# Third unit's rows loaded at the start, and quarters of the values projection between groups of transposes

## The chip, the cores and the metric

One core of a Trainium2 chip. The metric is the device time of one execution in microseconds; lower is better. PE is TensorE, DVE is VectorE, ACT is ScalarE, POOL is GpSimd, SP is SyncE, which here issues DMAs.

## The reference

Four layers on a sequence of 2048 rows of 640 numbers: attention, feed-forward, attention, feed-forward, with the same weights twice. All tensors are float32.

```python
def _A_ref(x, wqkv, wo):          # 32 heads of 20, window W = 256
    q, k, v = split heads of x @ wqkv
    scores = einsum("bhqd,bhkd->bhqk", q, k) * Dh ** -0.5
    scores = where(0 <= i - j < W, scores, -1e9)
    return merge heads of softmax(scores) @ v, then @ wo

def _B_ref(x, w1, b1, w2, b2):    # F = 1536
    r = relu(x @ w1 + b1)
    return (r * r) @ w2 + b2

x = x + _A_ref(layernorm(x)); x = x + _B_ref(layernorm(x))
x = x + _A_ref(layernorm(x)); x = x + _B_ref(layernorm(x))
```

## The kernel before

The sequence is cut into units of 256 rows (two blocks of 128), eight for each pair of layers, 16 in all, numbered u. Products are made from two float16 halves of each operand, in three matmuls (`mm3`): high by high, high by low, low by high.

For one unit the steps are these. `ln_load(u)` issues two loads of 128 rows from SP's queue and posts the layernorm's steps (statistics on DVE, the power on POOL, the scaling on DVE). `ln_t(u)` transposes the normalised rows on PE: `split_t` does one block in two groups, of three and two transposes of 128 columns, and each group is evicted by a cast on ACT (line 377) and a subtraction on DVE (line 378) into the two halves of yT. From the third unit's successors on another way is used (`ln_cross`, transposes by DMA). `stage_qk(u)` projects Q and K, evicts them on ACT and DVE (lines 507 and 510) and writes them to memory and back (lines 542 to 549), so that they come to lie by head pairs. `stage_v(u, which)` projects V in four quarters (two blocks by two halves of the columns), 15 matmuls each, and evicts each by one ACT instruction (line 580).

Attention goes in quads of four heads, eight for a unit. `max_quad` makes products and their row maxima (DVE, line 633), `max_out` transposes the maxima and sends them to rows of Q by DMA (lines 721 to 727, 689), `exp_quad` makes the products again with the maxima taken off, exponentials on ACT (line 779) and masks on POOL, and `pv_quad` multiplies by V. Maxima and exponentials use the same six PSUM banks, `bb`. `load_o(u)` fetches the result, and `stage_o` projects it (input `od`); `stage_f` is the feed-forward.

All other products share two PSUM buffers with the tag "mm" (`mm_tile`), so that a tile waits for the eviction of the tile before last.

The order on every engine is written by a planner in the kernel's own code. It keeps a clock for each engine; steps are generators that yield the time of what they put on PE, `post` and `dma` queue the work of the other engines with a cost and a priority (0 first), and `pump` puts what could start by then. A DMA is counted with its bytes over a rate (335, later 250 bytes per ns) behind all bytes counted so far. Weight loads issued by ACT (`bulk`) start when the counted backlog is under 2.2 us.

The first unit's attention is set out by `flow`: it goes through a list of maxima ("m"), rows ("r"), exponentials ("s") and products with V ("v"), and as long as the next entry isn't ready by the planner's clock, it takes a piece of the generator `rest`, which is `ahead_all()`. What `flow` has not used of `rest` is left for the second unit's part: 9 us of it by the planner's count are held back until the first `stage_o` has begun, for use between later steps.

The tiles with the tag "xt" (two buffers) hold the rows of a unit and, later, other rows. Those with the tag "x1" (two buffers) hold the input rows to which the first projection's result is added; `load_o` fills them (line 886). The second unit's yT lies in a part of the third K tile (`place`).

Of the kernel before, what the change touches and what calls it, by code (L numbers as in the profile page):

```python
# [10 lines left out]
F32 = mybir.dt.float32  # L11
# [5 lines left out]
P = 128  # L17
Q = P // 2
S = 2048
D = 640  # L20
# [25 lines left out]
def kernel(ctx: ExitStack, tc: tile.TileContext, x, wqkv, wo, w1, b1, w2, b2, out):  # L46
# [4 lines left out]
    sb = ctx.enter_context(tc.tile_pool(name="sb", bufs=1))  # L51
# [43 lines left out]
    def set_row(i, k):  # L95
        nc.vector.memset(krow[i][:, 512 * k:512 * (k + 1)], PAIR)
# [36 lines left out]
    def post(eng, cost, fn, *deps, wait=0.0, prio=1, **kw):  # L133

        j = Job(eng, cost, fn, [d for d in deps if d is not None], now[0] + wait, prio, **kw)
        k = len(pend)
        while k and pend[k - 1].prio > prio:
            k -= 1
        pend.insert(k, j)
        return j  # L140

    def bulk(fn, size, *deps, **kw):

        return post("A", 400.0, fn, *deps, prio=2, size=size, idle=True, land=WLAND, **kw)

    def dma(fn, size, *deps, n=1, cost=450.0, prio=1, **kw):

        return post("S", n * cost, fn, *deps, prio=prio, size=size, **kw)
# [18 lines left out]
    def need(*js):  # L167

        for j in js:
            while j.end is None:  # L170
                pass_time()
            now[0] = max(now[0], j.end)
# [55 lines left out]
    def mm_tile(shape, name):  # L228


        while len(banks2) > 1:
            empty = [b for b in banks2 if b and all(j.end is not None for j in b)]
            if empty:
                b = min(empty, key=lambda b: max(j.end for j in b))
                now[0] = max(now[0], max(j.end for j in b) + LAT)
                banks2.remove(b)
            else:
                pass_time()
        t = ps.tile(shape, F32, name=name, tag="mm", bufs=2)
        banks2.append([])  # L240
        return t, banks2[-1]
# [15 lines left out]
    def convert(st, hi, low, n, load, *deps, prio=2):  # L257

        a = post("A", 20 + 0.9 * n, lambda: nc.scalar.activation(hi, st, AF.Copy, scale=WS), load, *deps, prio=prio)
        return post("D", 30 + 1.04 * n, lambda: nc.vector.scalar_tensor_tensor(low, st, WS, hi, op0=ALU.mult,  # L260
                                                                               op1=ALU.subtract), a, prio=prio)
# [20 lines left out]
    def load_wo():  # L282

        v = wo.rearrange("(h c d) n -> d h c n", c=KC, d=4)
        raw = w2raw[:, (FC - KC) * D:].rearrange("p (c n) -> p c n", n=D)
        loads = []
        for d in range(4):
            loads.append(bulk(lambda d=d: nc.scalar.dma_start(raw[d * H:(d + 1) * H], v[d]), H * KC * D * 4, gate0))
        for c in range(KC):
            woj[c] = convert(raw[:, c], wo_s[:, 0, c], wo_s[:, 1, c], D, loads[-1], *loads[:-1])  # L290
        rowset[1] = [post("D", 460, lambda k=k: set_row(1, k), prio=2) for k in range(4)]
# [30 lines left out]
    def mm3(acc, lhs, rhs, nk, ns, then=None):  # L322

        k, t = 0, 0.0
        for c in range(nk):
            for a, b in ((0, 0), (0, 1), (1, 0)):
                nc.tensor.matmul(acc, lhs(a, c), rhs(b, c), start=(k == 0), stop=(k == 3 * nk - 1))  # L327
                k += 1
                t += ns
                if t >= STEP and k < 3 * nk:  # L330
                    yield t
                    t = 0.0
        if then is not None:
            then(t)
        yield t
# [31 lines left out]
                                                           op0=ALU.subtract, op1=ALU.mult), j, prio=prio)  # L367
        return j

    def split_t(y, dst, job, made, bb=None):  # L370


        yield Want(job, bank=False)
        need(job)

        def out(tr, jobs, c0, n, wait):
            j = post("A", 170 * n, lambda: nc.scalar.copy(dst[:, 0, c0:c0 + n], tr[:, :n]), wait=wait, prio=0)  # L377
            j = post("D", 170 * n, lambda: nc.vector.tensor_sub(dst[:, 1, c0:c0 + n], tr[:, :n], dst[:, 0, c0:c0 + n]), j,  # L378
                     prio=0)
            jobs.append(j)  # L380
            made.append(j)

        parts = []
        for k, (c0, n) in enumerate(((0, 3), (3, 2))):
            if bb is not None:
                tr, jobs = bb[:, k].rearrange("p (c n) -> p c n", n=P), bbjobs
            else:
                yield Want()
                tr, jobs = mm_tile([P, 4, P], "tr")
            for c in range(n):  # L390
                nc.tensor.transpose(tr[:, c, :], y[:, (c0 + c) * P:(c0 + c + 1) * P], ident)
            parts.append((tr, jobs, c0, n, 117 * n if bb is None else 117 * KC))
            if bb is None:
                out(*parts.pop())
                yield 117 * n
        if parts:
            for p in parts:
                out(*p)
            yield 117 * KC
# [3 lines left out]
    def xsrc(l, b):  # L403
        return x_rows[b * P:(b + 1) * P, :] if l == 0 else xs[b]
# [4 lines left out]

    lns = {}  # L410

    def ln_load(u, *deps, prio=2):

        l, g = divmod(u, NG)
        ys = []
        for i in range(2):
            xt = sb.tile([P, D], F32, name="xt", tag="xt", bufs=2)
            load = dma(lambda xt=xt, i=i: nc.sync.dma_start(xt, xsrc(l, 2 * g + i)), P * D * 4, *deps, prio=min(prio, 1))
            ys.append((xt, layernorm(xt, xt, load, prio=prio)))
        lns[u] = ys  # L420

    def ln_t(u, yT=None):
        ys = lns.pop(u)
        if yT is None:
            yT = sb.tile([P, 2, KC, T], F16, name="yT", tag="yT", bufs=1)
        yTs[u], pre[u] = yT, []
        bb = banks() if u == 0 else (None, None)
        for i in range(2):
            yield from split_t(ys[i][0], yT[:, :, :, i * P:(i + 1) * P], ys[i][1], pre[u], bb[i])

    def cross(ys, dst, room, prio=2):

# [34 lines left out]
    pre = {}  # L467
# [99 lines left out]
    def stage_v(u, which=range(4)):  # L567
        yT = yTs[u]
        for i in range(2):
            if u == 2:  # L570
                yield Want(sums[i], bank=False)
            vt = vts[(2 * u + i) % 6][0]
            for h in range(2):
                if 2 * i + h not in which:
                    continue
                yield Want()
                acc, jobs = mm_tile([P, 2 * T], "acc")
                need(*[wqj[c] for c in range((2 * D + h * HD) // P, (2 * D + (h + 1) * HD - 1) // P + 1)])
                def out(vt=vt, acc=acc, h=h):
                    nc.scalar.activation(vt[:, h * NP:(h + 1) * NP, 0:DH],  # L580
                                                 acc[:, :HD].rearrange("p (h d) -> p h d", d=DH),
                                                 AF.Copy, scale=1.0 / (YS * WS))

                yield from mm3(acc[:, :HD], lambda a, k: yT[:, a, k, i * P:(i + 1) * P],
                               lambda b, k: wq_s[:, b, k, 2 * D + h * HD:2 * D + (h + 1) * HD], KC, 136,
                               lambda wait: jobs.append(post("A", 320, out, wait=wait, prio=urgency["out"])))
# [11 lines left out]
    def banks():  # L598
        need(*bbjobs)
        bbjobs.clear()  # L600
        return bb6
# [251 lines left out]
    x1s, ys, y2s = {}, {}, {}  # L853
# [336 lines left out]

    spin(14)
    ln_load(0, prio=0)
    load_wq()
    run(ln_t(0))
    spin(7)
    rate[0] = 250.0
    ln_load(1)
    load_wo()
    load_w1()
    load_w2()  # L1200
# [3 lines left out]
    place = kts[2].rearrange("p a n -> p (a n)")[:, :2 * KC * T].rearrange("p (a c n) -> p a c n", a=2, n=T)  # L1204

    def ahead_all():
        yield from stage_qk(0)
        yield from stage_v(0, range(2))
        yield from ln_t(1, place)
        ln_load(2)  # L1210
        yield from stage_v(0, range(2, 4))
        yield from stage_qk(1)
        yield from ln_t(2)
        yield from stage_v(1)
        gate2.end = now[0]
        yield from stage_qk(2)
        yield from stage_v(2)

    rest = ahead_all()
    todo = [("m", n) for n in range(GQ)] + [("r", 0)] + [("m", n) for n in range(GQ, LEAD)]  # L1220
    for n in range(NQ):
# [61 lines left out]
```

## Time and profile before

| | |
|---|---|
| median of 3 runs | 1586.9 us (1585.45 to 1589.74) |
| profiled execution | 1589.08 us, span 1587.4 us |
| mean granted clock of PE | 0.997 |
| busy PE, DVE, ACT, POOL | 1556.4, 984.3, 733.9, 600.2 us |
| moved by DMA | 160.44 MB |

A line of the instructions in order of time gives the start, the time to the end of the group, engine, line, operation, output<-inputs, shape and count, and in brackets how long the engine was idle before and what ended that. In the busy time by stretch each engine's number in brackets is its count of instructions. Busy time counts instructions from start to end; a share over the whole span mixes stages that have different limits, so the stages are read one by one.

### The profile page before, as it was taken

The numbers are of one execution on the slowest core, as the hardware profiler recorded it, in microseconds if no ns is written. First come the engines' busy times: TensorE is split into PE (matmuls) and PEld (weight loads), VectorE is DVE, ScalarE is ACT, GpSimd is POOL, SyncE is SP. The second block draws the span as 40 slices with busy tenths as digits, with TensorE's granted clock in tenths as the row PEclk, the third lists the DMA queues.
The fourth block names the chain that finished last, engine by engine and source line by source line (L and its number), as shares of the span: only waits on it lengthen the run. The fifth ranks groups of instructions, "written<-read, shape, count | busy, mean of one in ns | idle before, by whom it ended". The sixth has DMA issues, their size and how long they took to land. (4 is left out here: it accounts for less than half of the span.)

```text
span 1587.4 us, 52465 instructions
## 1 busy us (share of the span) xinstructions
PE 1556.4 (98%) x21534; PEld 1167.0 (74%) x21534; DVE 984.3 (62%) x3253; ACT 733.9 (46%) x1593; POOL 600.2 (38%) x1291
## 2 busy tenths in 40 slices
PE   8989999999999999999999999999999999999999
PEld 7666767777777777778777777777777777776767
DVE  8777665656756656665566656557665666756431
ACT  4555445444453444535343453544545345454612
POOL 1234434234252433525323352442535235253612
PEclk9999999999999999999999999999999999999999
DMA  9864344362533525354352534434343353431120
GB/s 265 208 181 105 77 110 87 101 128 52 121 87 106 108 61 133 70 125 86 97 132 59 119 87 116 98 88 110 71 123 83 98 117 69 107 87 58 29 67 18
DMA packets 243209, 160.44 MB, mean 101 GB/s; under 512 B 91160, under 2 KB 226712, under 8 KB 242968
## 3 DMA queue, kind: packets, MB, share of 16 engines
q1 hardware_dynamic: 236600, 147.58, 39.3%
q10 hardware_dynamic: 6368, 9.50, 2.1%
q8 instruction: 169, 2.77, 0.8%
q14 instruction: 72, 0.59, 0.1%
HBM read 84.68 MB, written 52.95 MB: 87 GB/s over the span
## 5 line engine op out<-in xcount | busy, mean ns | idle before, releaser
L779 ACT ACTIVATE pt<-bb 128x512 f32<-128x512 f32 (+1 forms) x736 | 375.9, 601 | 226.4 <-PE bb L757 203.2
L633 DVE CUSTOM_DVE_ANT_0 bb<-bb,maskq 128x320 f32<-128x320 f32 x896 | 409.3, 523 | 89.7 <-PE bb L653 76.1
L794 POOL TENSOR_SCALAR_AFFINE_SELECT pt<-pt 128x256 f32<-128x256 f32 x448 | 188.6, 423 | 564.1 <-ACT pt L779 550.9
L327 PE MATMUL acc<-y,w_s 128*128 128x256 f16 x2880 | 330.0, 274 | 2.5 <-ACT y L377 1.4
L327 PE MATMUL acc<-w_s,hh 128*128 128x320 f16 x2304 | 326.0, 299 | 0.0
L327 PEld LDWEIGHTS <-w_s 128*128 128x128 f16 x2880 | 277.3, 98 | 55.2 <-issue 17.9
L327 PEld LDWEIGHTS <-hh 128*128 128x128 f16 x2304 | 220.6, 98 | 98.1 <-issue 11.5
L327 PEld LDWEIGHTS <-wq_s 128*128 128x128 f16 x2400 | 229.5, 98 | 46.5 <-issue 13.9
L327 PE MATMUL acc<-yT,wq_s 128*128 128x256 f16 x2250 | 258.7, 273 | 2.7 <-DVE qd L510 1.3
L798 POOL TENSOR_SCALAR_AFFINE_SELECT pt<-pt 128x256 f32<-128x256 f32 x512 | 213.6, 439 | 90.5 <-ACT pt L779 88.8
L1013 DVE TENSOR_TENSOR hh<-r,hh 128x256 f16<-128x256 f32 x192 | 95.0, 517 | 211.1 <-ACT hh L1010 204.1
L828 PE MATMUL pv<-pt,vt 128*32 128x128 f32 (+1 forms) x3840 | 190.1, 331 | 1.2 <-POOL pt L798 1.2
L1007 POOL TENSOR_TENSOR r<-r 128x256 f32<-128x256 f32 x192 | 114.3, 616 | 162.1 <-ACT r L1003 159.8
L840 ACT COPY ot<-pv 128x256 f32<-128x256 f32 x128 | 47.6, 372 | 269.3 <-PE pv L828 269.3
L327 PE MATMUL acc<-wo_s,od 128*128 128x320 f16 x960 | 140.4, 302 | 5.0 <-ACT od L911 3.0
L633 DVE DVE_READ_ACCUMULATOR2_ANT mx<- 128x1 f32 x1024 | 142.7, 139 | 0.0
L828 PEld LDWEIGHTS pv<-pt,vt 128*32 128x32 f32 x3840 | 105.2, 110 | 41.5 <-POOL pt L798 7.2
L327 PE MATMUL acc<-wq_s,yT 128*128 128x320 f16 x900 | 131.8, 299 | 1.0 <-DVE y L378 0.5
L327 PEld LDWEIGHTS <-od 128*128 128x128 f16 x960 | 91.6, 98 | 50.2 <-issue 6.4
L1003 ACT ACTIVATE r<-acc,b1s 128x256 f32<-128x256 f32 x192 | 80.5, 471 | 89.4 <-PE acc L327 88.1
L327 PEld LDWEIGHTS <-yT 128*128 128x128 f16 x900 | 85.7, 98 | 38.9 <-issue 6.3
L364 POOL TENSOR_TENSOR bmv<-bmv,neghalf 128x1 f32<-128x1 f32 x64 | 44.9, 708 | 137.4 <-DVE bmv L358 136.9
(95 smaller groups left out, 1224.4 us busy)
## 6 DMA issues: line engine op xcount, KB each, us to landing
qt<-qk SPq DMA_DIRECT2D x30, 480.0 KB
kt<-qk SPq DMA_DIRECT2D x30, 480.0 KB
qk<-qd SPq DMA_DIRECT2D x17, 640.0 KB
o<-ot SPq DMA_DIRECT2D x256, 42.0 KB
od<-o SPq DMA_DIRECT2D x14, 640.0 KB
qk<-yl SPq DMA_DIRECT2D x13, 640.0 KB
qk<-qd SPq DMA_DIRECT2D x17, 320.0 KB
xt<-in_A_x_dram SPq DMA_DIRECT2D x16, 320.0 KB
```

Source lines behind the costliest of these rows:

```text
L327: nc.tensor.matmul(acc, lhs(a, c), rhs(b, c), start=(k == 0), stop=(k == 3 * nk - 1))
L364: j = post("G", 520, lambda: nc.gpsimd.tensor_tensor(box["mv"][:, 3:4], box["mv"][:, 2:3], neghalf, op=ALU.pow), j, prio=prio)
L633: nc.vector.tensor_tensor_reduce(out=v, in0=v, in1=mask, scale=1.0, scalar=-3.0e38, op0=ALU.add, op1=ALU.max, accum_out=accum[e, w]),
L779: nc.scalar.activation(box["pt"][:, :o], bb[e][:, k, :o], AF.Exp, scale=SCALE / (QS * QS))
L794: nc.gpsimd.affine_select(out=m, in_=m, pattern=[[0, 2], [-1, P]], compare_op=ALU.is_gt, fill=0.0, base=0, channel_multiplier=1)
L798: nc.gpsimd.affine_select(out=m, in_=m, pattern=[[0, 2], [1, P]], compare_op=ALU.is_ge, fill=0.0, base=0, channel_multiplier=-1)
L828: nc.tensor.matmul(pv[32 * jj:32 * (jj + 1), q0 * P:(q0 + qn) * P], vf[:, c:c + 32], pj[:, j, :], start=(k == 0), stop=(k == len(steps) - ...
L840: nc.scalar.copy(ot[:, qd % 2], pv)
L1003: nc.scalar.activation(box["r"], acc[:, f, :], AF.Relu, bias=b1s[:, f0 + f:f0 + f + 1], scale=1.0 / (YS * WS))
L1007: nc.gpsimd.tensor_tensor(box["r"], box["r"], box["r"], op=ALU.mult)
L1013: nc.vector.tensor_sub(hh[:, 1, f, :], box["r"], hh[:, 0, f, :])
```

## The change

`split_t` gets a list of generators, `between`, and runs one behind each group of transposes. `ln_t` hands two of the list to each block. `ln_load` takes the tag of its tiles. The third unit's rows (u = 2) are loaded directly after the second's, into the tiles with the tag "x1", and their layernorm is posted there. In `ahead_all` only the first quarter of the first unit's values stands ahead of the second unit's transposes; the other three stand between these, and the four quarters of the second unit's values stand between and behind the third unit's transposes.

```diff
--- before.py
+++ after.py
@@ -367,7 +367,7 @@
                                                            op0=ALU.subtract, op1=ALU.mult), j, prio=prio)
         return j
 
-    def split_t(y, dst, job, made, bb=None):
+    def split_t(y, dst, job, made, bb=None, between=()):
 
 
         yield Want(job, bank=False)
@@ -393,6 +393,8 @@
             if bb is None:
                 out(*parts.pop())
                 yield 117 * n
+                for g in between[k:k + 1]:
+                    yield from g
         if parts:
             for p in parts:
                 out(*p)
@@ -409,24 +411,24 @@
 
     lns = {}
 
-    def ln_load(u, *deps, prio=2):
+    def ln_load(u, *deps, prio=2, tag="xt"):
 
         l, g = divmod(u, NG)
         ys = []
         for i in range(2):
-            xt = sb.tile([P, D], F32, name="xt", tag="xt", bufs=2)
+            xt = sb.tile([P, D], F32, name="xt", tag=tag, bufs=2)
             load = dma(lambda xt=xt, i=i: nc.sync.dma_start(xt, xsrc(l, 2 * g + i)), P * D * 4, *deps, prio=min(prio, 1))
             ys.append((xt, layernorm(xt, xt, load, prio=prio)))
         lns[u] = ys
 
-    def ln_t(u, yT=None):
+    def ln_t(u, yT=None, between=()):
         ys = lns.pop(u)
         if yT is None:
             yT = sb.tile([P, 2, KC, T], F16, name="yT", tag="yT", bufs=1)
         yTs[u], pre[u] = yT, []
         bb = banks() if u == 0 else (None, None)
         for i in range(2):
-            yield from split_t(ys[i][0], yT[:, :, :, i * P:(i + 1) * P], ys[i][1], pre[u], bb[i])
+            yield from split_t(ys[i][0], yT[:, :, :, i * P:(i + 1) * P], ys[i][1], pre[u], bb[i], between[2 * i:2 * i + 2])
 
     def cross(ys, dst, room, prio=2):
 
@@ -1195,6 +1197,7 @@
     spin(7)
     rate[0] = 250.0
     ln_load(1)
+    ln_load(2, tag="x1")
     load_wo()
     load_w1()
     load_w2()
@@ -1205,13 +1208,10 @@
 
     def ahead_all():
         yield from stage_qk(0)
-        yield from stage_v(0, range(2))
-        yield from ln_t(1, place)
-        ln_load(2)
-        yield from stage_v(0, range(2, 4))
+        yield from stage_v(0, range(1))
+        yield from ln_t(1, place, [stage_v(0, [k]) for k in (1, 2, 3)])
         yield from stage_qk(1)
-        yield from ln_t(2)
-        yield from stage_v(1)
+        yield from ln_t(2, None, [stage_v(1, [k]) for k in range(4)])
         gate2.end = now[0]
         yield from stage_qk(2)
         yield from stage_v(2)
```

## Prediction

> **What bounds the kernel now.** I read the page's totals first, then the busy time by stretch, and only then the instructions in order of time, where the stretches left something to find.
>
> ```profile
> span 1587.4 us, 52465 instructions
> PE 1556.4 (98%) x21534; PEld 1167.0 (74%) x21534; DVE 984.3 (62%) x3253; ACT 733.9 (46%) x1593; POOL 600.2 (38%) x1291
> ```
> ```profile
> 30.00:70.00 40.00, 35.03 (x336) 24.98 (x335) 31.67 (x130) 19.15 (x42) 7.49 (x15) 1.00 0.82 204
> 70.00:105.00 35.00, 32.09 (x418) 22.14 (x418) 24.38 (x88) 20.99 (x45) 9.26 (x20) 1.00 0.75 208
> 105.00:125.00 20.00, 14.76 (x155) 10.16 (x155) 17.86 (x52) 7.38 (x16) 4.75 (x8) 0.83 0.79 182
> ...
> 250.00:1350.00 1100.00, 1099.98 (x15642) 828.59 (x15634) 681.42 (x2271) 511.55 (x1116) 433.50 (x942) 1.00 0.42 97
> ```
>
> The columns are the stretch and its length, then the busy time of PE, PEld, DVE, ACT and POOL, the granted clock, the DMA share and GB/s. Over the 1100 us from 250 on PE is idle for 0.02 us: nothing can be won there. The change acts between 30 and 105, where PE is idle for 4.97 + 2.91 us. Behind it lies the worst stretch, 105 to 125: 5.24 us idle and a mean clock of 0.83. These three hold 13.1 us of idle time, 0.8% of the span, and that caps what an edit here can bring, apart from the clock.
>
> The instructions of PE in order of time (start, duration, idle before) show who ends the waits:
>
> ```profile
> 32.39 0.49 PE L668 MATMUL bb<-kt,qt 60*128 60x128 f16 x7 [1.32 <-DMA kt<-qk]
> ...
> 34.59 0.44 PE L391 MATMUL tr<-ident,xt 128*128 128x128 f32 x2 [0.33 <-ACT vt L580]
> 35.59 0.80 PE L391 MATMUL tr<-ident,xt 128*128 128x128 f32 x5 [0.56 <-DVE kt L378]
> ...
> 37.30 2.74 PE L327 MATMUL acc<-wq_s,yT 128*128 128x320 f16 x19 [0.47 <-DVE kt L378]
> ...
> 47.36 0.49 PE L765 MATMUL bb<-qt,kt 62*128 62x256 f16 x7 [0.75 <-DVE bmv L357]
> ...
> 61.66 0.50 PE L765 MATMUL bb<-qt,kt 62*128 62x256 f16 x8
> ...
> 68.03 0.44 PE L391 MATMUL tr<-ident,xt 128*128 128x128 f32 x2 [0.56 <-DVE qd L510]
> 68.70 1.12 PE L391 MATMUL tr<-ident,xt 128*128 128x128 f32 x5 [0.24 <-DVE yT L378]
> 70.83 0.70 PE L327 MATMUL acc<-wq_s,kt 128*128 128x320 f16 x4 [1.00 <-DVE yT L378]
> 71.46 0.50 PE L765 MATMUL bb<-qt,kt 62*128 62x256 f16 x8
> ...
> 85.73 1.25 PE L327 MATMUL acc<-yT,wq_s 128*128 128x256 f16 x10 [0.53 <-ACT vt L580]
> ...
> 113.45 0.33 PE L653 MATMUL bb<-kt,qt 60*64 60x256 f16 x1 [1.94 <-ACT pt L779]
> ...
> 119.81 0.45 PE L327 MATMUL acc<-wo_s,od 128*128 128x320 f16 x2 [2.31 <-ACT od L911]
> ```
>
> Two things happen at once here. The planner fills PE with projections (the dense work), and between them runs the first unit's attention, a chain of latencies: the first maxima at 32.39 wait for the K tile to land, the first exponentials run at 47.36, and so on until the output projection finds its input at 119.81. Up to there PE waits at the end for the chain, and the planner holds a fixed amount of the third unit's projection back until the output projection has begun. So the work left at 119.81 is about the same however PE spent its time before, and **the end of the kernel moves by what that 119.81 moves**, plus the clock. A stall taken out of the dense work ahead of it only makes PE arrive sooner at that wait.
>
> **The stalls at the transposes.** A tile of PSUM waits for the eviction of the tile before last. In the second unit's transposes the waits are 0.33 + 0.56 + 0.47 = 1.36 us. With value quarters between, each group of transposes has some 2 us of matmuls (a quarter) to hide its cast and subtraction, so its own wait goes. A quarter that follows two or three transposes then waits for the quarter before them, whose one eviction by ACT the short transposes don't cover: the nearest rows are 0.33 above and this one:
>
> ```profile
> 137.88 0.44 PE L391 MATMUL tr<-ident,xt 128*128 128x128 f32 x2 [0.20 <-ACT vt L580]
> ```
>
> I take 0.26 for each of three. The list for unit 1 has three quarters for four groups, so its last group stands bare before the next projection, which needs it: the row of 70.83 has that case at 1.00. Together 0.78 + 1.00 = 1.78, worse than before by 0.42 (bounds: 0.2 x 3 if an attention step falls into the last gap, -0.76; 0.33 x 3 + 1.00, +0.63). For unit 2 four quarters follow four groups. Before: 0.56 + 0.24 + 1.00 and the 0.53 at 85.73, 2.33. After: the 0.56 for the last Q/K eviction stays, and three times 0.26: 1.34, so -0.99 (bounds -1.2 and -0.78). Sum of both: -0.57 us of PE idle time, which by the argument above is not yet time gained.
>
> **The rows of the third unit.** The two loads move from behind the second unit's transposes to directly behind the second unit's loads.
>
> ```profile
> 15.47 1.49 SPq L418 DMA_DIRECT2D xt<-in_A_x_dram  x2
> 17.05 0.52 SPq L542 DMA_DIRECT2D qk<-qd  x1
> ...
> 25.37 0.84 SPq L548 DMA_DIRECT2D qt<-qk  x2
> 26.30 0.91 SPq L548 DMA_DIRECT2D kt<-qk  x2
> ...
> 36.83 1.20 SPq L418 DMA_DIRECT2D xt<-in_A_x_dram  x2
> 40.88 2.88 SPq L689 DMA_DIRECT2D qt<-mT  x4
> ```
> ```profile
> xt<-in_A_x_dram SPq DMA_DIRECT2D x16, 320.0 KB
> ```
> ```profile
> 20.00:22.00 2.00, 2.00 (x21) 1.79 (x19) 1.88 (x4) 0.72 (x2) 0.00 (x0) 1.00 1.06 375
> ...
> 24.00:26.00 2.00, 2.00 (x21) 1.79 (x20) 2.00 (x5) 0.60 (x1) 0.00 (x0) 1.00 0.49 152
> ...
> 38.00:46.00 8.00, 7.78 (x69) 5.93 (x67) 5.96 (x34) 0.99 (x3) 0.00 (x0) 1.00 1.03 244
> ```
>
> On SP's queue they are moved ahead of the first unit's writes and reloads of Q and K, the rows of the maxima not included. 655 KB at the 375 GB/s of a full stretch are 1.75 us; two issues cost SP 1.49 us. So the write at 17.05 is issued at about 18.5 and lands some 1.9 us later, the reloads at 25.37 and 26.30 too, and the first maxima go from 32.39 to 34.3. Bounds: 0.75, if the half-empty 2 us at 24 to 26 take up 1 us; and 2.6, because the planner counts these bytes at 250 per ns and places the attention by that. I take 1.9, since each step waits for the one before to land and the gap at 24 lies behind the delayed write.
>
> What comes back: at 36.83 the same bytes no longer stand ahead of the rows of maxima issued at 40.88, through engines that are full (1.03) from 38 to 46. Between 0 and 1.75; I take 1.0.
>
> The Trainium skill ("DMA: Bandwidth & Descriptors", section "Issuing engines are not separate DMA queues") has SP's and ACT's transfers on the same 16 engines, interleaved, so ACT's weight loads would fill the freed room. By that rule nothing comes back here, the chain gains 0.3 instead of the 1.3 below, the clock term below falls away, and the time is 1586.6.
>
> Then the DVE queue, in order of time:
>
> ```profile
> 34.99 0.91 DVE L378 TENSOR_TENSOR kt<-tr,kt 128x384 f16<-128x384 f32 x2
> ...
> 53.62 0.61 DVE L366 TENSOR_SCALAR xt<-xt,bmv 128x640 f32<-128x640 f32 x1
> ```
>
> The first row stands between the reductions of the first maxima. With these 1.9 us later, two of the four groups are evicted ahead of them: -0.9 (bounds 0 and -0.9). So the first exponentials stay at 47.36: +1.9 - 1.0 - 0.9 = 0.0.
>
> The third unit's layernorm moves from between the maxima to about 30 us, where DVE waits for the first maxima, longer once these are late (it is idle for 8.3 of the 40 us from 30 to 70); its last step above stood where the second quad's exponentials begin. -0.3 (bounds 0 and -0.61). Its rows land at about 26 us, ahead of the second unit's own last statistics on DVE, so nothing is queued behind a late load. The tiles it uses are first needed for the output's rows long after: no wait is added.
>
> **The third unit's transposes in the chain.** From the exponentials at 61.66 to those at 71.46 take 9.8 us; the same step from 78.61 to 83.77 takes 5.2:
>
> ```profile
> 78.61 0.49 PE L765 MATMUL bb<-qt,kt 62*128 62x256 f16 x7 [0.59 <-DMA qt<-mT]
> ...
> 83.77 0.83 PE L765 MATMUL bb<-qt,kt 62*128 62x256 f16 x8
> ```
> ```profile
> 61.70:71.50 9.80, 7.77 (x74) 4.93 (x75) 8.98 (x28) 5.44 (x13) 2.70 (x4) 1.00 0.88 191
> 78.60:83.80 5.20, 5.19 (x55) 3.21 (x56) 2.38 (x15) 3.67 (x8) 1.53 (x4) 1.00 0.91 173
> ```
> ```profile
> 61.70:71.50 9.80, 1.86 (x4) 1.00 0.88 191
> ```
>
> DVE is busy for 8.98 of the 9.8 us, and 1.86 of it are the four subtractions behind the transposes (the last row is line 378 alone). Quarters between them push two of the four out of this step, into one where DVE has room: -1.0 (bounds 0 and -1.86). Sum for the chain: 0.0 - 0.3 - 1.0 = -1.3 us, so the 119.81 becomes 118.5. With all bounds at one end it is -4.4 (0.75 - 0.9 - 1.75 - 0.61 - 1.86), at the other +2.6.
>
> **The clock.** Behind both long gaps the granted clock is down:
>
> ```profile
> 112.00:118.00 6.00, 3.90 (x70) 2.44 (x69) 4.43 (x9) 2.28 (x6) 3.80 (x8) 0.72 0.92 249
> 120.00:124.00 4.00, 3.73 (x16) 2.04 (x15) 4.00 (x16) 0.61 (x2) 0.00 (x0) 0.57 1.15 222
> ```
>
> 6 x 0.28 and 4 x 0.43 us are lost, 1.7 each, behind gaps of 1.94 and 2.31 us; the gap of 1.32 at 32.39 is followed by a clock of 1.00. So a gap somewhere under 1.94 us costs only itself. The last gap becomes 2.31 + 0.57 (PE arrives sooner) - 1.3 = 1.6 us, and its dip goes: -1.7. The Trainium skill ("TensorE: Matmul & The Clock Gate", section "What's actually happening") has the clock fall after an idle window of about 3.4 us; by that neither gap would have cost clock and there were nothing to win, 1585.6. The trace disagrees: 1.94 us did it.
>
> **Sum**: -1.3 - 1.7 = -3.0. The profiled execution took 1589.08 us (span 1587.4 and 1.7 around it), 2.2 above the median of the three runs; it would be 1586.1, and the median goes from 1586.9 to **1583.9 us**. That is 0.19%, under the 0.3% (4.8 us) that a measurement of this kernel can tell from no change.
>
> **Rivals.**
> *The chain shortens by more.* The gap at 24 to 26 takes up 1 us, the freed room goes to the maxima, both subtractions and the layernorm leave the step: about -3.0 of the possible -4.4, both gaps fall under the limit, and both dips go: -3.0 - 3.4 = -6.4, 1580.5. For it: each term has a row. Against it: the gap at 113.45 waits for exponentials of the second unit, which nothing here touches.
> *The stalls move and nothing else.* PE idle time shrinks early and grows by as much at 119.81; delay and returns cancel: 1586.9.
> *The rows ahead of Q and K decide: slower.* The first maxima come 2.6 us late, as the planner books it, nothing comes back, and their gap grows from 1.32 past 1.94, which costs a dip of 1.7. With the bare last group of unit 1 inside the chain (0.42 to 0.63) that is +4.9, 1591.8. It decides from about 2 us of net delay at the first exponentials. For it: each hop at 17 to 32 waits for the one before. Against it: PE has the quarters to run meanwhile.
> *It does not do what it says*: the loads would have to wait for their tiles; the first use of these tiles is at load_o, so hardly.
>
> **Chances.** Forecast 0.33; stalls only moved 0.15; not doing what it says 0.02; shorter chain 0.29; slower 0.21. The first three lie within 0.3%: same 0.50, faster 0.29, slower 0.21. The range goes past the shorter chain's 1580.5 by 1 us and to the slower rival's 1591.8: 1579.5 to 1592.0, which leaves out a tenth on each side. The forecast's own range is 1582 to 1587.
>
> **What would show it.** In the profile after: the loads of the third unit at about 17 us on SP and the first Q write at 18.5; the first maxima near 34.3; transposes with no wait of their own and quarters with 0.2 to 0.3 <-ACT vt; a wait of about 1 us before the second unit's Q projection; the first exponentials within 1 us of 47.4; the output projection at about 118.5, with no dip of the clock behind it. I am wrong if the output projection moves and the end doesn't follow, if the first exponentials are over 1.5 us late, or if idle time appears behind 250 us, where there is none now.

## The result, and the profile after

The changed kernel is slower: 1594.03 us (median of 10 runs, 1591.53 to 1596.1) against 1587.56 us (10 runs, 1585.28 to 1591.57), a ratio of 1.0041 with an interval of 1.0032 to 1.0051. Forecast were 1583.9 us and a range up to 1592.0. The profiled execution took 1594.85 us, 5.8 more than that of before, and its span is 5.7 us longer:

```profile
span 1593.1 us, 52469 instructions
PE 1558.6 (98%) x21534; PEld 1168.4 (73%) x21534; DVE 985.2 (62%) x3253; ACT 733.8 (46%) x1593; POOL 598.9 (38%) x1291
```

PE is idle for 34.5 us instead of 31.0, and 2.2 us longer busy with the same 21534 matmuls: more of them ran at a lower clock. The busy time by stretch (the columns as in the prediction) shows where:

```profile
30.00:70.00 40.00, 34.12 (x320) 24.34 (x317) 28.23 (x112) 17.26 (x37) 7.56 (x14) 0.96 0.70 172
70.00:105.00 35.00, 32.77 (x387) 22.91 (x387) 26.18 (x102) 17.58 (x41) 9.23 (x20) 1.00 0.70 187
105.00:125.00 20.00, 14.45 (x195) 9.61 (x194) 15.49 (x45) 11.96 (x24) 4.96 (x10) 0.85 0.75 206
125.00:150.00 25.00, 20.45 (x249) 13.83 (x247) 18.93 (x56) 11.97 (x25) 8.30 (x19) 0.98 0.54 141
...
250.00:1350.00 1100.00, 1099.97 (x15651) 828.39 (x15649) 682.18 (x2272) 513.28 (x1120) 433.85 (x943) 1.00 0.43 97
```

Between 250 and 1350 us nothing changed. The granted clock is 0.96 between 30 and 70, where it was 1.00 (40 x 0.04 = 1.6 us), and 125 to 150 holds 4.55 us of idle time, where before it held 1.25:

```profile
125.00:150.00 25.00, 23.75 (x336) 16.74 (x335) 19.12 (x62) 13.83 (x28) 9.29 (x19) 1.00 0.35 113
```

The instructions of PE in order of time, after:

```profile
30.53 2.20 PE L327 MATMUL acc<-wq_s,yT 128*128 128x320 f16 x15 [0.20 <-ACT vt L582]
...
36.61 0.50 PE L670 MATMUL bb<-kt,qt 60*128 60x128 f16 x8
...
43.10 0.27 PE L723 MATMUL tr<-ident,mx 128*16 128x128 f32 x1
...
50.44 0.27 PE L767 MATMUL bb<-qt,kt 62*128 62x256 f16 x1 [1.61 <-DMA qt<-mT]
52.12 0.49 PE L767 MATMUL bb<-qt,kt 62*128 62x256 f16 x7 [1.41 <-DMA qt<-mT]
...
60.13 0.70 PE L327 MATMUL acc<-kt,wq_s 128*128 128x256 f16 x5 [1.39 <-DVE qd L512]
...
66.58 0.50 PE L767 MATMUL bb<-qt,kt 62*128 62x256 f16 x8
...
73.79 0.57 PE L767 MATMUL bb<-qt,kt 62*128 62x256 f16 x8
...
121.62 0.45 PE L327 MATMUL acc<-wo_s,od 128*128 128x320 f16 x2 [2.19 <-ACT od L913]
...
130.00 0.28 PE L723 MATMUL tr<-ident,mx 128*16 128x128 f32 x1 [1.33 <-DVE x L941]
...
143.48 0.75 PE L759 MATMUL bb<-qt,kt 62*64 62x192 f16 x31 [0.97 <-DVE mx L635]
...
147.74 0.44 PE L391 MATMUL tr<-ident,xt 128*128 128x128 f32 x2 [1.04 <-ACT vt L582]
```

The first maxima run at 36.61 instead of 32.39, and without a wait: the planner put them there. Seven of the eight products of the first exponentials run at 52.12 instead of 47.36, behind 3.0 us of waiting for the rows of maxima. The clock does not fall there: from 30 to 60 us it is 1.00. It falls behind the next gap, the 1.39 us ahead of 60.13:

```profile
52.00:54.00 2.00, 1.88 (x21) 1.66 (x22) 0.29 (x1) 1.30 (x3) 0.41 (x1) 1.00 0.28 89
60.00:66.00 6.00, 5.87 (x50) 3.93 (x50) 5.32 (x22) 4.94 (x10) 2.21 (x4) 0.72 0.12 33
```

The step from 66.58 to 73.79, with the interleaved transposes in it, takes 7.2 us instead of 9.8, so by the output projection at 121.62 only 1.8 us of the delay are left. Then new waits follow (130.00, 143.48, 147.74), and the feed-forward starts at 153.0 instead of 147.5: 3.6 of the 5.4 us arise behind the start of the output projection. SP's queue, and the weight loads that ACT issues, after and (last fence) before:

```profile
14.74 2.45 SPq L420 DMA_DIRECT2D xt<-in_A_x_dram  x4
...
28.13 0.38 SPq L544 DMA_DIRECT2D qk<-qd  x1
...
29.04 2.35 SPq L550 DMA_DIRECT2D kt<-qk  x2
...
43.72 3.81 SPq L691 DMA_DIRECT2D qt<-mT  x4
```
```profile
38.98 0.69 ACTq L288 DMA_DIRECT2D w_s<-in_A_wo_dram  x1
39.71 1.26 ACTq L288 DMA_DIRECT2D w_s<-in_A_wo_dram  x2
44.51 0.57 ACTq L288 DMA_DIRECT2D w_s<-in_A_wo_dram  x1
45.11 0.61 ACTq L297 DMA_DIRECT2D w_s<-in_B_w_dram  x1
```
```profile
33.36 0.69 ACTq L288 DMA_DIRECT2D w_s<-in_A_wo_dram  x1
...
47.98 0.41 ACTq L297 DMA_DIRECT2D w_s<-in_B_w_dram  x1
```

The first reload of K stands in SP's queue behind the last write of Q now (28.13) and is issued at 29.04 instead of 26.30. ACT's weight loads start 5.6 us later (38.98 instead of 33.36), and so the first five, one of w1 among them (45.11), are issued between 38.98 and 45.7, around the rows' four transfers (43.72 to 47.5). Before, the first load of w1 came at 47.98, when the rows had landed.

### The profile page after: what moved, and what is told of

The parts are those of the page before. It is cut to its first block, busy times and chain, and to the rows that moved or that the text cites. A ratio compares the mean times of both kernels' runs of the same rounds, so it can differ in the third digit from the quotient of the medians.

```text
span 1593.1 us, 52469 instructions
## 1 busy us (share of the span) xinstructions
PE 1558.6 (98%) x21534; PEld 1168.4 (73%) x21534; DVE 985.2 (62%) x3253; ACT 733.8 (46%) x1593; POOL 598.9 (38%) x1291
## 5 line engine op out<-in xcount | busy, mean ns | idle before, releaser
L327 PEld LDWEIGHTS <-wq_s 128*128 128x128 f16 x2400 | 229.7, 98 | 47.3 <-issue 14.4
```

## The experiments

Every kernel was run five rounds beside the kernel before. The ratios come from those runs; a profile is one execution and shows the places, and its time can stand up to 4 us from the median of the same kernel. A difference of 1 or 2 us at one place is therefore compared, below, over several profiles with the same plan up to there.

The theories: **A1**, the planner's booking of the early load pushes the first attention back; **A2**, the bytes themselves do; **B**, the quarters between the transposes are the loss; **D**, weight loads stand ahead of the rows of maxima; **X**, the late input rows of the output projection; **C**, any other plan than that of before is slower; **Q**, ACT's in-order wait for the write of Q. D, X and C were formed after the first group of runs, Q after the third.

In the table, "late step" is the start of the third unit's third exponentials, behind which all kernels repeat the same work. It tells the end of the profiled execution within 2 us in every profile. The columns give the start of the first of eight products; 32.39, 47.36 and 52.12 in the text are the starts of the other seven, behind a wait.

| kernel | ratio (interval) | first maxima | first exponentials | late step |
|---|---|---|---|---|
| before | 1 | 30.8 | 46.3 | 230.9 |
| the change | 1.0041 (1.0032 to 1.0051) | 36.6 | 50.4 | 236.1 |
| e1 early load alone | 1.0049 (1.0037 to 1.0062) | 36.2 | 49.8 | 237.9 |
| e2 quarters alone | 1.0065 (1.0051 to 1.0079) | 31.7 | 45.4 | 240.3 |
| e3 quarters of the second unit alone | 1.0018 (1.0009 to 1.0027) | 31.2 | 45.2 | 232.4 |
| e5 change, load behind Q and K | 1.0077 (1.0064 to 1.0090) | 31.1 | 46.4 | 241.9 |
| e6 change, load not booked | 1.0050 (1.0037 to 1.0063) | 32.2 | 47.2 | 236.2 |
| e7 change, input rows early | 1.0072 (1.0059 to 1.0085) | 36.7 | 50.1 | 239.8 |
| e8 change, w1 held | 1.0136 (1.0122 to 1.0150) | 36.7 | 51.1 | 247.9 |
| e9 before, booking alone | 1.0091 (1.0076 to 1.0107) | 35.9 | 48.0 | 241.8 |
| e11 before, input rows early | 1.0016 (1.0008 to 1.0025) | 31.3 | 45.9 | 231.9 |
| e12 change, w1 and w2 held | 1.0029 (1.0017 to 1.0040) | 36.6 | 49.5 | 231.3 |
| e13 early load alone, not booked | 1.0086 (1.0072 to 1.0100) | 30.8 | 46.9 | 246.0 |
| p1 before, rate 260 | 1.0075 (1.0062 to 1.0088) | 30.5 | 44.8 | 241.7 |
| f1 rate 260, K apart | 1.0053 (1.0039 to 1.0067) | 30.6 | 45.1 | 234.3 |
| f2 before, K apart | 0.9995 (0.9985 to 1.0005) | 31.1 | 45.6 | 230.6 |
| f3 change, w1 and w2 held, K apart | 1.0020 (1.0012 to 1.0029) | 36.6 | 49.7 | 232.0 |
| f4 before, w1 and w2 held | 1.0000 (0.9991 to 1.0009) | 31.2 | 46.7 | 232.1 |
| f5 e13, K apart | 1.0054 (1.0040 to 1.0067) | 31.0 | 47.0 | 236.5 |
| g1 e2, K apart | 1.0027 (1.0015 to 1.0038) | 31.1 | 44.5 | 233.2 |

### Each half alone

e1 takes the early load and leaves the order; e2 takes the order and leaves the load:

```diff
 # e1, against the change
-        yield from stage_v(0, range(1))
-        yield from ln_t(1, place, [stage_v(0, [k]) for k in (1, 2, 3)])
+        yield from stage_v(0, range(2))
+        yield from ln_t(1, place)
+        yield from stage_v(0, range(2, 4))
         yield from stage_qk(1)
-        yield from ln_t(2, None, [stage_v(1, [k]) for k in range(4)])
+        yield from ln_t(2)
+        yield from stage_v(1)
 # e2, against the change
-    ln_load(2, tag="x1")
...
         yield from ln_t(1, place, [stage_v(0, [k]) for k in (1, 2, 3)])
+        ln_load(2)
         yield from stage_qk(1)
```

> The third unit's rows are loaded at the start as in the changed kernel; the quarters of the values stand as before. Theory A (the early load pushes the first unit's attention back and that is the loss): 4 to 6.5 us slower than before, first maxima at 35 to 37 us on PE, first exponentials at 50 or later. Theory B (the quarters between the transposes are the loss): within 1.5 us of before.

> The quarters stand between the transposes as in the changed kernel; the third unit's rows are loaded where they were before, into the tiles of before. Theory A: not slower than before, 0 to 3 us faster, first maxima at 32.4, first exponentials at 47 to 48, the step over the third unit's transposes shorter by 1 to 2.5 us. Theory B: 4 to 6.5 us slower.

Measured 1.0049 and 1.0065, 7.8 and 10.3 us: neither theory holds as it stood. A foretold the places of e1, B foretold that e2 is slower, both times lie above the 4 to 6.5 us foretold, and each half costs at least as much as both. In e2 the first exponentials come earlier than before; the loss is at the third quad, where PE waits 3.69 us for an exponential, and ACT for a transfer:

```profile
64.34 0.76 PE L670 MATMUL bb<-kt,qt 60*128 60x128 f16 x8 [3.69 <-ACT pt L781]
```
```profile
58.51 1.07 ACT L781 ACTIVATE pt<-bb 128x512 f32<-128x512 f32 x2
63.42 0.60 ACT L509 ACTIVATE qd<-acc 128x512 f16<-128x512 f32 x1 [3.83 <-DMA qk<-qd]
63.91 0.66 ACT L781 ACTIVATE pt<-bb 128x256 f32<-128x256 f32 x2
```
```profile
52.72 2.75 SPq L691 DMA_DIRECT2D qt<-mT  x4
55.57 2.00 SPq L847 DMA_DIRECT2D o<-ot  x4
57.67 0.39 SPq L544 DMA_DIRECT2D qk<-qd  x1
```

Q and K of one unit are evicted into the same staging tile. K's eviction waits until Q is written out, and the two last exponentials of the quad stand behind it on ACT. Here Q's write stands on SP behind the rows of maxima and the attention's output and is issued at 57.67; before, it stood ahead of both:

```profile
54.59 0.38 SPq L542 DMA_DIRECT2D qk<-qd  x1
...
55.66 3.79 SPq L689 DMA_DIRECT2D qt<-mT  x4
```

### Where the load stands, and what the planner books for it

e5 posts the load behind `stage_qk(0)`; e6 books 16 KB for the two transfers instead of 655 KB.

```diff
 # e5
-    ln_load(2, tag="x1")
...
         yield from stage_qk(0)
+        ln_load(2, tag="x1")
 # e6
-    ln_load(2, tag="x1")
+    ln_load(2, tag="x1", counted=8192)
```

> The changed kernel, but the third unit's loads are posted behind the first unit's Q and K projection, so that SP issues them behind the first writes of Q and K; they still go to the empty tiles. Theory A: first maxima back at 32 to 34 us, time within 1.5 us of before or up to 3 us faster. Theory B: 4 to 6.5 us slower, as with the change.

> The changed kernel, but the planner books only 16 KB instead of 655 KB for the third unit's loads; the transfers themselves stay. If the planner's booking is what pushes the first attention (A1): first maxima placed as before, PE waits there for K until about 34.3, and half or more of the 6.5 us come back. If the bytes themselves do it (A2): first exponentials at 50 or later all the same and over 4 us slower than before. Theory B: no different from the change.

Both put the first maxima back to 31 to 33 us, as A and A1 have it, and neither gave time back (1.0077 and 1.0050). In e6 seven products of the first exponentials ran at 50.76 although the maxima came early, PE waiting 3.33 us for the rows: what A1 gives back, the rows take. That the cause is D is not shown for this plan, since no run holds the weights in it.

e9 is the counterpart: the booking alone, in the kernel before, with no byte moved. e13 is the early load alone without the booking.

```diff
 # e9, against the kernel before
     ln_load(1)
+    post("S", 0.0, lambda: None, prio=1, size=2 * P * D * 4)
 # e13, against e1
-    ln_load(2, tag="x1")
+    ln_load(2, tag="x1", counted=8192)
```

> The kernel before, with one entry in the planner added that books 655 KB behind the second unit's loads and moves no byte. Theory A1 (the booking pushes the first attention and the weight loads): first maxima placed at 35 to 37 us, first exponentials at 49 to 52, 4 to 7 us slower than before. Theory A2 (the bytes themselves): within 1.5 us of before, first maxima at 33 to 35 because of the planner, without a wait.

> The early load alone, order of the quarters as before, and the planner books only 16 KB for it, so that the plan stays nearly that of before while the bytes do go ahead of the first unit's Q and K. Theory A1 (the booking is the loss): within 2 us of before; PE waits for the first K tile until 33.5 to 34.5 instead of 32.4, which comes back by the first exponentials or costs 1 to 2 us. Theory A2 (the bytes): 4 to 8 us slower, like the early load with booking (1.0049).

The first maxima tell A1 from A2. With the booking alone (e9, first line) they go to 35.89. With the bytes alone (e13, second line) they run at 32.40 behind a wait for the K tile:

```profile
35.89 0.50 PE L668 MATMUL bb<-kt,qt 60*128 60x128 f16 x8
```
```profile
32.40 0.49 PE L670 MATMUL bb<-kt,qt 60*128 60x128 f16 x7 [1.36 <-DMA kt<-qk]
```
```profile
31.07 0.50 PE L668 MATMUL bb<-kt,qt 60*128 60x128 f16 x8
```

The profile of before has nearly the same as e13 (32.39, behind 1.32 us), but it is the exception. In the four other kernels with its plan up to here and without the early bytes (e3, e11, f4, and f2 in the third line) the first maxima run at 31.07 to 31.32 without a wait; in the three with the early bytes and no booking (e13, f5, e6) at 32.40 to 33.04, behind waits of 1.3 to 1.5 us. So the 655 KB ahead of Q and K cost the first K tile some 1.3 us, an estimate from these profiles, and the number in the planner 3.5 us against the profile of before and 4.7 against the other four. In the changed kernel PE does not wait for the K tile at all: the booking sets the place.

The times, 1.0091 and 1.0086 (14.4 and 13.7 us), are both worse than the change, and worse than A1 (4 to 7) and A2 (4 to 8) foretold. In e13 ACT waits 3.5 us at 63 for Q's write, as in e2. Without the booking, w1's first load is issued 4.7 us earlier than in the kernel before (43.23), and Q's write stands behind other transfers (61.10 instead of 54.59).

### The rows of maxima and the weight loads

e8 holds w1's loads until the rows of the first maxima have landed in the planner's account, e12 w1's and w2's. f4 does the same in the kernel before.

```diff
 # e8: gate1 ends with the first rows; e12 adds it to w2's loads as well
-                st, w1[...]...), P * KC * 2 * P * 4, gate,
+                st, w1[...]...), P * KC * 2 * P * 4, gate, gate1,
...
+        if u == 0 and G == 0:
+            rowjobs[u, G].gates.append(gate1)
```

> The changed kernel, but the loads of w1 by ACT also wait, in the planner, for the rows of the first maxima. Theory D (the rows stand in the DMA engines behind weight loads that now fall together with them): the first exponentials' second half goes from 52.1 to 48 to 50.5 us, the chain follows by as much, and 1.5 to 3.5 us of the time come back. Theory A1 (only the late placing of the first maxima): first exponentials near 52 still, no change of the time over 1 us.

> The changed kernel with both w1 and w2 held, in the planner, until the rows of the first maxima have landed; with w1 alone held, w2 had slipped into its place. Theory D: four rows' loads land within 7 us of the transposed maxima (9.0 with the change), first exponentials' second half at 48.5 to 50.5 instead of 52.1, and PE's gap there shrinks from 3.0 to under 1.5 us. The whole time can still be worse, as w1 comes later. Against D: still at 52.

e8 failed as an experiment: w2's loads took the room at once (at 45.2 and 47.9), so the rows landed hardly earlier (seven products of the first exponentials at 51.9 instead of 52.1), and the plan behind put 19.2 us of the feed-forward's second product in one piece at 179.5. The attention left over then stood alone: PE was busy 11 of the 20 us from 200. e12 did what D foretold. Up to the first exponentials it differs from the change in one load of w1, issued at 47.77 instead of 45.11. The seven products start 6.9 us after the maxima are transposed (9.0 with the change, 7.1 before), and PE waits 0.9 instead of 3.0 us:

```profile
49.55 0.27 PE L769 MATMUL bb<-qt,kt 62*128 62x256 f16 x1 [0.73 <-DMA qt<-mT]
49.98 0.49 PE L769 MATMUL bb<-qt,kt 62*128 62x256 f16 x7 [0.17 <-DMA qt<-mT]
```

Two more profiles bear it out: e7, with the plan of the change, has 8.8 us here, and f3, which holds the weights too, 7.1. The ratio falls from 1.0041 to 1.0029; the intervals overlap, so the time alone doesn't show it, the place does. In e12 the output projection then starts earlier than in the kernel before (119.81):

```profile
117.23 0.45 PE L327 MATMUL acc<-wo_s,od 128*128 128x320 f16 x2 [2.54 <-ACT od L915]
```

The feed-forward starts at 148.1 all the same, 0.6 us later than before.

> The kernel before with w1 and w2 held behind the rows of the first maxima. There the rows land 6.5 us after the transposed maxima were split and the weight loads come behind them anyway, so theory D has nothing to mend: within 2 us of before. Theory C: 2 us or more slower.

1.0000: where no load of w1 or w2 stands ahead of the rows, holding them mends nothing, by D. C, which wanted 2 us or more, is wrong here. In f4's profile, though, 8.9 us pass from the transposed maxima to the seven products, with the held loads behind the rows: the weight loads are not the only thing that can delay the rows, and what did it here is open.

### The input rows of the output projection

e7 and e11 load them without waiting for the attention's result, in the changed kernel and in the kernel before:

```diff
-                load_x(i, *([loaded] if u == 0 else wrote if u == NU - 1 else ()))
+                load_x(i, *(wrote if u == NU - 1 else ()))
```

> The changed kernel, but the two loads of input rows for the first output projection are posted without waiting for the attention's result, so that they land before 115 us. In the changed kernel DVE waits 1.3 us for them at 129 us, with the transposed maxima queued behind it, and the feed-forward starts 5.5 us later than before although the output projection starts only 1.8 us later. If this wait starts the rest of that delay (theory X): the output projection stays near 121.6, the feed-forward starts at 149.5 to 151.5 instead of 153.0, and 1.3 to 3.7 us come back. If the delay is only a matter of the order behind it: under 1 us.

> The kernel before, with the same early load of the input rows for the first output projection. There DVE waits 0.8 us for them. Theory X: 0 to 1.5 us faster. Theory C (any other plan of the first 150 us costs, since the order before is a lucky one): 2 us or more slower.

DVE's wait is gone in both, and both are slower than without the edit (1.0072, 1.0016). In e7 PE waits 2.48 and 2.70 us for exponentials at 123 and 140 instead. X's price couldn't be measured in this way: the edit moves the plan. That e11 is slower at all speaks for C, against X.

### How sensitive the plan is

p1 changes one number of the planner and no work. e3 interleaves only the third unit's transposes, so that the plan up to them stays.

```diff
 # p1
-    rate[0] = 250.0
+    rate[0] = 260.0
 # e3, against the kernel before
-        yield from ln_t(2)
-        yield from stage_v(1)
+        yield from ln_t(2, None, [stage_v(1, [k]) for k in range(4)])
```

> The kernel before, with nothing changed but the planner's assumed transfer rate in the first 120 us, 260 instead of 250 bytes per ns. No work is added or taken out. Theory C (the order before is a chance optimum among plans): 1 to 6 us slower. If the plan is robust: within 1 us.

> The kernel before with only the third unit's transposes and the second unit's four quarters interleaved; loads as before, so that nothing changes before 66 us. If this interleaving is good in itself (the step of the prediction: 1 us of the chain, 1 us of stalls): 0 to 3 us faster. If the plan behind it is what decides (C): 1 to 6 us slower, with a wait of ACT for a transfer behind 66 us that the kernel before doesn't have.

A rate 4% higher costs 0.75%, nearly twice what the change costs, and twice the most that C foretold. The trace has the same sign as e2's: ACT waits 3.6 us at 62 for Q's write, issued at 59.6. e3 costs 0.18%; the step from the third to the fourth exponentials falls to 8.1 us (60.5 to 68.6, 9.8 before), as the prediction had it, and ACT then waits 4.1 us for Q's write, this time the third unit's, as C has it.

### A staging tile for K

Theory Q says that this wait is the common cause of the variants' losses. In the changed kernel itself it is small: 0.95 us at 104, as against 1.45 before. The first unit's K already has a tile of its own; f1, f2, f3, f5 and g1 give it to the second unit's too:

```diff
-                if j and u == 0:
+                if j and u < 2:
```

> The kernel before with the planner's rate at 260 (1.0075 by itself), and the second unit's K evicted into a staging tile of its own, so that ACT needn't wait until Q has been written out. Theory Q (ACT's in-order wait of 3.6 us at 62 to 66 for the write of Q, with two exponentials behind it, is the loss): the wait is gone, and at least 4 of the 12.8 us come back. Otherwise: less than 2 us come back.

> The quarters between the transposes alone (1.0065), and the second unit's K in a staging tile of its own. Theory Q: ACT's 3.8 us wait at 59 to 63 for Q's write is gone, the step from the third quad's exponentials to the next maxima takes 3 us instead of 6.5, and at least 4 of the 10.3 us come back. Otherwise under 2.

> The early load alone, not booked (1.0086), and the second unit's K in a staging tile of its own. Theory Q: ACT's 3.5 us wait at 63 to 67 is gone and at least 5 of the 14.4 us come back. If the early bytes are otherwise free, the rest is within 3 us of before.

In g1 the exponentials follow each other on ACT, and the maxima come 2.8 us after the exponentials instead of 6.5:

```profile
57.57 1.07 ACT L781 ACTIVATE pt<-bb 128x512 f32<-128x512 f32 x2
58.65 0.60 ACT L509 ACTIVATE stg<-acc 128x512 f16<-128x512 f32 x1
59.14 0.66 ACT L781 ACTIVATE pt<-bb 128x256 f32<-128x256 f32 x2
```

From 1.0065 to 1.0027 for the quarters alone (6.0 us of 10.3), from 1.0086 to 1.0054 for the early bytes (5.1 of 13.7), and from 1.0075 to 1.0053 for the rate (3.5 of 11.9, where 4 were expected and the intervals overlap). The rest of f5, 8.6 us, is more than the 3 us expected, so the wait at the second unit's K is not all of it. The same wait at the third unit's K is still there, 3.3 us long as in e13; for that K the tile isn't free, since the attention's result is loaded into it.

> The kernel before with the second unit's K in a staging tile of its own. Before has no wait of ACT for Q's write at that place (only 1.4 us for the third unit's at 104), so by theory Q no gain: within 2 us of before, unless the plan changes; by theory C 2 us or more slower.

> The changed kernel with w1 and w2 held behind the rows of the first maxima (1.0029) and the second unit's K in a staging tile of its own. In the held kernel ACT waits only 0.9 us for Q's write. Theory Q: 0 to 2 us better than the held kernel, 1.002 to 1.003. By theory C anything from there to 1.008.

f2 is level with before (0.9995): there the wait was hidden already. f3 brings the change to 1.0020, below the change's interval: the two edits together bring back 3.3 of its 6.5 us. Their parts are not told apart: e12's interval overlaps both. No version was clearly faster than the kernel before.

## Why the prediction was wrong

**The transposes' stalls** were right in kind and too small. After, the waits in the second unit's interleaving are 0.20, 0.31 and 0.20, in the third's 0.32, 0.20 and 0.31; the bare last group cost no 1.00, since maxima were put behind it (these waited 0.52 and 0.17 us for DVE at 39.45 instead). That is 1.54 us instead of 3.69, 2.15 less where 0.57 were forecast. A new wait for an eviction, 1.39 us at 60.13, lies outside the transposes. The time went up all the same; that such a stall isn't time as long as the chain decides fits this, but no run shows it alone.

**The early rows: the first step that failed.** I charged 1.9 us to the bytes and kept the planner's 2.6 as a bound. It was the other way round: the planner's booking decides. e9 shows 3.5 us for it and e13, with two other profiles, about 1.3 for the bytes, which in the changed kernel nothing waits for. Why the booking costs more than its 2.6 us isn't shown; in e9 and in the changed kernel alike the reload of K also stands behind one more write of Q on SP. A sign in the prediction's list fails with it: the first write of Q was to be issued at 18.5, it was at 17.29, and over all profiles it lies between 16.2 and 18.9, with the early rows and without. The wait of 1.32 us at 32.39, on which this step was built, is in one profile of five with that plan.

**"What comes back: 1.0" had the wrong sign.** I saw room in the queue at 36.83 and gave it to the rows. The loads that wait for room are the weights', which start when the planner's backlog is small and which the same delay had pushed into these microseconds. The rows took 9.0 us instead of 7.1. The rule of the Trainium skill ("DMA: Bandwidth & Descriptors", section "Issuing engines are not separate DMA queues"), weighed and set aside in the prediction, was the better guide here: SP's rows and ACT's weights shared the engines, and e12 shows it by holding the one (6.9 us instead of 9.0). Its 1586.6 was too low as well, because it was taken for room filled, not for a new queue.

**The DVE steps** had the right sign and were too small, the second beyond its bound of -1.86: from the first maxima to their transposition 6.5 us instead of 7.9 (forecast -0.9), over the third unit's transposes 7.2 instead of 9.8 (forecast -1.0). So the sum at the first exponentials was +4.8 where 0.0 stood, and at the output projection +1.8 where -1.3 stood.

**"The end moves by what 119.81 moves": the second step that failed,** and the larger in size. The output projection came 1.8 us late, 3.1 off the forecast; the end came another 3.9 us late where 1.7 were to be won, 5.6 off. e12 shows it without the delay: its output projection starts at 117.23, 2.6 us earlier than before, its feed-forward 0.6 us later. The plan between the two is what changed. The waits at 143.48 and 147.74, 0.97 and 1.04 us with the change, are of the same length in e12 and f3, where all of it runs about 5 us earlier, and 0.21 and 0.26 us before and in f2: they come with the order, not with the delay. Ahead of them the output projection brought its own late transfer: its input rows were issued at 120.91 instead of 116.82, behind the reloads of the third unit's Q, DVE waited 1.3 us for them (0.8 before), and the transposed maxima stood behind it on DVE. DVE's order, after and before, shows where the wait at 143.48 comes from:

```profile
140.03 0.82 DVE L260 SCALAR_TENSOR_TENSOR w_s<-vt,w_s 128x640 f16<-128x640 f32 x1 [0.19 <-ACT w_s L259]
...
142.08 0.89 DVE L378 TENSOR_TENSOR y<-tr,y 128x384 f16<-128x384 f32 x2
142.88 0.49 DVE L635 CUSTOM_DVE_ANT_0 bb<-bb,maskq 128x320 f32<-128x320 f32 x1
```
```profile
138.18 0.53 DVE L633 CUSTOM_DVE_ANT_0 bb<-bb,maskq 128x320 f32<-128x320 f32 x1
138.63 0.88 DVE L378 TENSOR_TENSOR y<-tr,y 128x384 f16<-128x384 f32 x2
```

Before, all reductions of these maxima stand ahead of the transposes' subtractions (line 378). With the change the conversion of a late weight load stands among them and the subtractions ahead of the last one, for which the products at 143.48 wait. Likewise six exponentials instead of four stand on ACT ahead of the eviction for which 147.74 waits. No run changes this order alone, so what each of these waits costs at the end is open; e7 didn't settle it.

**The clock**: the dips behind the gaps of 1.94 and 2.19 us stayed, and a third came at 60 to 66, 6 x 0.28 = 1.7 us, the size given in the prediction. The limit between 1.32 and 1.94 us doesn't hold: this dip follows a gap of 1.39, while e12 has a gap of 1.36 at 57.98 and a clock of 1.00 from 50 to 66. e7, whose plan is the same up to there, has its third dip at 52 to 58, behind the rows' gap:

```profile
52.00:58.00 6.00, 6.00 (x57) 3.93 (x57) 1.81 (x10) 2.47 (x7) 1.54 (x4) 0.72 0.67 212
```

So with late rows (the change, e7) a third dip came, at one gap or the other, and with the weights held (e12, f3) none. What decides where it falls isn't shown.

**The slower rival** had part of the mechanism (maxima late by the booking, nothing back) at a chance of 0.21 and a price of 4.9 us; 6.5 were measured. That its price is near is partly luck: its dip was to follow the gap ahead of the first maxima, which is gone, its bare last group cost nothing, and the 3.9 us behind the output projection aren't in it.

## What to carry to other kernels

In a kernel whose order comes from its own planner, an edit's first cost is what it changes in the planner's account: list every decision that reads that account (here the placing of dependent work and the start of background loads), and follow each into the queue where it lands. Before an in-order engine is given work that waits for a transfer, look at what stands behind it: one staging tile shared by two products put exponentials behind a write for 3.5 to 3.8 us in three different plans (e2, e13, p1), and waits of that kind over 3 us stand in four more (e3, e5, e9, f5). A rule of the form "the end moves by what this point moves" needs the same plan behind the point. And test the plan's sensitivity first, by a neutral number such as a rate: if that alone moves the time by more than the edit promises, a forecast from the old trace carries that width.

## What the runs showed that was not expected

A profile of the same plan can differ by more than 1 us at a place: the kernel before waits 1.32 us for the first K tile, four other kernels with its plan up to there not at all. Booking 655 KB in the planner delayed the first maxima by 3.5 us or more, moving these bytes delayed them by about 1.3. A planner's rate changed by 4% cost 0.75%, and a booking without a transfer 0.91%. Two plans that differ from that of before (f2, f4) are as fast as it is, so the kernel before isn't the only good plan, but 16 of the 18 variants tried are slower, by 0.16 to 1.36%.
